# Moving one 128-column copy out of PSUM from ScalarE to VectorE in the opening of a layernorm, state-space and gated-MLP kernel

## The chip, the cores and the metric

One core of one Trainium2 chip. The metric is the device time of the kernel in microseconds (us). Each timed comparison runs a kernel and the kernel before in turn on the same chip. A ratio is the mean time of one kernel's fast runs over the mean of the other's of the same rounds, with a 95% interval, so it is not quite the ratio of the medians quoted beside it. "Same" means within 2%.

## The reference

2048 rows of 512 bf16 values are normalised; the result feeds a diagonal state-space layer (A) and a gated MLP (B), and everything is added to the input.

```python
def _B_ref(x, w_gate, w_up, w_down):
    return (_gelu(x @ w_gate) * (x @ w_up)) @ w_down
x = A_x
xn = _layernorm(x, axis=-1)
return x + _A_ref(xn, ...) + _B_ref(xn, B_w_gate, B_w_up, B_w_down)
```

## The kernel before

The kernel builds a list of operations with estimated durations; a list scheduler orders VectorE, ScalarE and GpSimd by them, while TensorE and the sync queue run in the order of the program. The change lies in the first 5 us. To start TensorE early, the kernel doesn't normalise the first three tiles of 128 rows before the gate and up products. It subtracts a mean ("centring"), turns the centred tile by TensorE transposes into PSUM, copies it to SBUF, multiplies, and applies the scale afterwards. A tile's first turn (128 columns) has its own copy, so that the products of weight block k = 0 can start before the other three turns.

```python
def cent_T(j, k0, k1, bank):
    pt = PS[bank].bitcast(BF16)[:, 0:128 * (k1 - k0)]
    ...                                                # f: TensorE transposes of XN[j] into pt
    PE(f, 56.0 * (k1 - k0), [XNp[j][k0 > 0] if j < 2 else XN[j], IDN], [BANK[bank]], "T0")
    ...
    GATE["evTA"] = ACT(lambda e: e.activation(dst, src, ACTF.Copy), ...)     # the copy, on ScalarE
...
ch(cent(0, 0), cent(0, 1))         # VectorE, tile 0 (ch: keep this order on the engine)
cent_T(0, 0, 1, 7)                 # first turn of tile 0 and its copy
ch(cent(1, 0), cent(1, 1))         # VectorE, tile 1
fill(1)                            # one filler matmul
cent_T(0, 1, 4, 5)                 # the other three turns of tile 0
ks(0, 0, [0], True)                # gate products, block 0, tile 0
cent_T(1, 0, 1, 6)                 # first turn of tile 1
ks(0, 0, [1])                      # up products, block 0, tile 0
cent_T(1, 1, 4, 7)
ks(0, 1, [0], True); ks(0, 1, [1])
```

The weights come in blocks of 128 KB on the sync queue: gate 0, up 0, gate 1, up 1 and so on. Activation tiles 1 and 2 come on ScalarE's queue meanwhile.

## Time and profile before

| | before |
|---|---|
| median of the three runs known at first | 177.22 us (176.98 to 177.30) |
| profiled run, its span | 176.79 us, 175.5 us |
| TensorE / VectorE / ScalarE busy | 98% / 91% / 55% |

The span runs from the first to the last instruction. The prediction shows the engines' line, the chain of waits of the opening and the copy. Two more rows, from the page's 40 equal slices (4.4 us each): the granted TensorE clock in tenths, and the busy share of the 16 DMA engines.

```profile
PEclk9999999999999999999999999999999999999999
DMA  5999999794996000002025000002001000000321
```

The DMA engines are busy nine tenths or more in nine of the eleven slices from the second to the twelfth, and a finer view of this trace gives a busy share of 0.99 to 1.05 for each microsecond from 2 to 5 us, though whether the loads slow each other there is not shown. The clock row shows nothing but nines, although the first matmuls are twice as far apart as the later ones (427 against 216 ns for 512 columns); the starts of the matmuls have to be read for that. Below, "half clock" and "full clock" mean these two paces, and "release" the change from the first to the second.

### The profile page before, as it was taken

Reading aid. Unit: us, or ns where it says so; the run is one execution under the profiler, and the core shown is the slowest. Engines: PE = TensorE matmul, PEld = TensorE weight load, DVE = VectorE, ACT = ScalarE, POOL = GpSimd, SP = SyncE. Lnnn points to the kernel's source line nnn. Section 1 sums busy time; section 2 is a strip of 40 time slices with the busy share of each in tenths; the row PEclk is TensorE's granted clock in tenths of the full one; section 3 lists DMA queues with packets and bytes.
Section 4 is the critical chain, followed back from the end, with each engine's and each line's share of the span. In section 5 each row is a group of like instructions: output and inputs, shape, how many; then the busy total and the mean of one; then the engine's idle time right before and its main releaser. Section 6 shows DMA issues by size and latency. Waiting matters only on the chain.

```text
span 175.5 us, 2521 instructions
## 1 busy us (share of the span) xinstructions
PE 172.7 (98%) x889; PEld 84.9 (48%) x889; DVE 159.6 (91%) x279; ACT 95.9 (55%) x187; POOL 10.7 (6%) x24
## 2 busy tenths in 40 slices
PE   8999999999999999999999999999999999999995
PEld 2646464845544444444644444444454444444453
DVE  5987999997989989799899999989999899999931
ACT  5476778999767898484576792000667960000000
POOL 3212220220000000002100000000000000000000
PEclk9999999999999999999999999999999999999999
DMA  5999999794996000002025000002001000000321
GB/s 173 258 326 198 206 191 166 137 136 95 235 299 170 4 0 2 0 30 90 4 50 102 0 0 0 4 0 90 30 0 30 4 0 0 0 0 0 99 87 58
DMA packets 32420, 14.36 MB, mean 82 GB/s; under 512 B 23736, under 2 KB 32408, under 8 KB 32408
## 3 DMA queue, kind: packets, MB, share of 16 engines
q1 hardware_dynamic: 32096, 13.94, 35.0%
q10 hardware_dynamic: 312, 0.27, 0.6%
q8 instruction: 7, 0.11, 0.3%
q14 instruction: 5, 0.04, 0.1%
HBM read 6.46 MB, written 2.10 MB: 49 GB/s over the span
## 4 chain that ended last, share of the span: by engine, by line
PE 98%; DVE 0%; issue 0%
PE PS L880 37%; PE PS L839 32%; PE PS L745 16%; PE PS L708 4%; PE PS L697 3%; PE PS L813 3%; PE PS L929 2%; PE PS L680 1%; DVE arena L898 0%; PE PS L936 0%
## 5 line engine op out<-in xcount | busy, mean ns | idle before, releaser
L880 PE MATMUL PS<-arena 128*128 128x512 bf16 (+3 forms) x323 | 66.2, 366 | 0.0
L839 PE MATMUL PS<-arena 128*128 128x512 bf16 x264 | 58.1, 379 | 0.0
L880 PEld LDWEIGHTS PS<-arena 128*128 128x128 bf16 (+1 forms) x323 | 30.8, 98 | 35.2
L839 PEld LDWEIGHTS PS<-arena 128*128 128x128 bf16 x264 | 25.8, 98 | 30.2
L783 DVE TENSOR_TENSOR_SCAN arena<-arena 128x512 bf16<-128x512 f32 x32 | 38.8, 1252 | 0.0
L854 ACT ACTIVATE arena<-PS 128x512 bf16<-128x512 f32 x33 | 19.8, 599 | 26.2 <-DVE arena L898 16.7
L745 PE MATMUL PS<-arena 128*128 128x512 bf16 (+1 forms) x144 | 28.2, 355 | 0.0
L858 ACT ACTIVATE arena<-PS 128x512 bf16<-128x512 f32 x33 | 19.8, 599 | 5.4 <-PE PS L839 5.4
L745 PEld LDWEIGHTS PS<-arena 128*128 128x128 bf16 x144 | 14.1, 98 | 13.3
L872 ACT ACTIVATE PS<-arena 128x512 f32<-128x512 bf16 (+2 forms) x17 | 9.6, 581 | 19.7 <-DVE arena L898 19.0
L754 ACT ACTIVATE arena<-PS 128x512 bf16<-128x512 f32 x32 | 17.5, 595 | 1.8 <-PE PS L745 1.8
L898 DVE TENSOR_TENSOR arena<-PS,arena 128x512 bf16<-128x512 f32 (+2 forms) x17 | 10.9, 652 | 6.4 <-PE PS L880 6.3
L860 DVE TENSOR_TENSOR arena<-arena 128x512 bf16<-128x512 bf16 x33 | 13.1, 415 | 2.3 <-ACT arena L858 2.0
L772 DVE TENSOR_TENSOR arena<-arena 128x4096 bf16<-128x4096 bf16 (+1 forms) x5 | 9.2, 1857 | 0.4 <-ACT arena L607 0.4
L795 DVE TENSOR_TENSOR arena<-arena 128x4096 bf16<-128x4096 bf16 x4 | 9.2, 2290 | 0.1
L770 DVE TENSOR_TENSOR arena<-arena 128x4096 bf16<-128x4096 bf16 (+1 forms) x5 | 9.2, 1856 | 0.0
L796 DVE TENSOR_TENSOR arena<-arena 128x4096 bf16<-128x4096 bf16 x4 | 9.1, 2285 | 0.0
L717 ACT ACTIVATE arena<-PS,arena 128x256 bf16<-128x256 f32 (+1 forms) x16 | 6.5, 449 | 4.1 <-PE PS L697 2.4
L611 DVE BATCH_NORM_STATS2 arena<-arena 128x6 f32<-128x512 bf16 x12 | 7.7, 680 | 0.1
L708 PE MATMUL PS<-arena 128*128 128x512 bf16 (+1 forms) x40 | 7.1, 336 | 0.0
L720 DVE SCALAR_TENSOR_TENSOR arena<-PS,arena 128x256 bf16<-128x256 f32 (+1 forms) x16 | 6.3, 443 | 0.4 <-PE PS L697 0.4
L697 PE MATMUL PS<-arena 128*128 128x512 bf16 (+1 forms) x30 | 6.3, 350 | 0.0
(95 smaller groups left out, 124.2 us busy)
## 6 DMA issues: line engine op xcount, KB each, us to landing
out_dram<-arena SPq DMA_DIRECT2D x15, 128.0 KB, 1.7
arena<-in_A_x_dram SPq DMA_DIRECT2D x3, 512.0 KB, 5.8
arena<-in_B_w_down_dram SPq DMA_DIRECT2D x1, 1280.0 KB, 7.1
arena<-in_B_w_gate_dram SPq DMA_DIRECT2D x4, 128.0 KB, 3.1
arena<-in_B_w_up_dram SPq DMA_DIRECT2D x4, 128.0 KB, 3.4
arena<-in_B_w_gate_dram SPq DMA_DIRECT2D x1, 480.0 KB, 6.4
arena<-in_B_w_up_dram SPq DMA_DIRECT2D x1, 480.0 KB, 7.2
arena<-arena SPq DMA_TRANSPOSE x25, 3.1
```

The lines of the kernel that those rows point to most:

```text
L697: PE(lambda e: e.matmul(dst, XCd(j, k), WGU[:, ws[0]:ws[-1] + 1, k, f0:f1], start=first, stop=k == KD - 1, skip_group_check=True), d_pe([w ...
L708: ins_ = e.matmul(dst, XCd(j, k), WGU[:, :, k, f0:f1], start=(k == 0), stop=(k == KD - 1))
L745: ins_ = e.matmul(PS[bank][:, 128 * j0:128 * j1], BBT[c][dk].ap[:, 128 * s:128 * (s + 1)], XNT[b].ap[:, dk, 128 * j0:128 * j1], start=(dk ...
L754: GATE["evBu"] = ACT(lambda e, bank=bank, k3=k3, s=s, c=c: e.activation(SSc[k3][s][c].ap, PS[bank][:, :], ACTF.Copy), d_act(512), [BANK[ba ...
L783: V(lambda e, g=g, rb=rb, init=init: e.tensor_tensor_scan(g.ap, rb, g.ap, init, ALU.mult, ALU.add), d_dve_scan(512), [g, PA[RRr]] + ([CARc ...
L839: ins_ = e.matmul(PS[bank][0:m, c0:c1], W.ap[:, dk, 128 * ft:128 * ft + m], XNT[b].ap[:, dk, c0:c1], start=(dk == 0), stop=(dk == KD - 1))
L854: GATE["last_gelu"] = ACT(lambda e, bg=bg, kk=kk, m=m: e.activation(GG[kk].ap[0:m, :], PS[bg][0:m, :], ACTF.Gelu_apprx_tanh), d_act(512), ...
L858: ACT(lambda e, bu=bu, kk=kk, m=m: e.activation(UPB[kk].ap[0:m, :], PS[bu][0:m, :], ACTF.Copy), d_act(512), [BANK[bu]], [UPB[kk]], "evU")
L860: V(lambda e, kk=kk, m=m, ft=ft, k2=k2: e.tensor_tensor(HTt[k2][ft].ap[0:m, :], GG[kk].ap[0:m, :], UPB[kk].ap[0:m, :], ALU.mult), d_dve_tt ...
L872: ACT(lambda e: e.activation(PS[bank][:, c0:c1], X[tt].ap[:, c0:c1], ACTF.Copy), d_act(c1 - c0), [X[tt]], [BANK[bank]], "seed")
L880: ins_ = e.matmul(PS[bank][:, c0:c1], l_[:, 128 * j:128 * (j + 1)], r_[:, c0:c1], start=False, stop=last and n == len(ops) - 1, skip_group ...
L898: V(lambda e: e.tensor_tensor(OUTB[ko].ap[:, c0:c1], PS[bank][:, c0:c1], XD[tt].ap[:, c0:c1], ALU.add), d_dve_1x(c1 - c0), [BANK[bank], XD ...
```

## The change

The intent: the first turn's copy stands between TensorE and its first useful product. VectorE is expected to do it sooner (the kernel's own estimates, which are constants in its code, are 187 ns against 297 on ScalarE), and it goes into VectorE's queue ahead of the centring of tile 1, not behind it.

```diff
-        def cent_T(j, k0, k1, bank):
+        def cent_T(j, k0, k1, bank, eng="A"):
...
+            if eng == "V":
+                return V(lambda e: e.tensor_copy(dst, src), 110 + 0.6 * 128 * (k1 - k0), [BANK[bank]], w, "evT")
             GATE["evTA"] = ACT(lambda e: e.activation(dst, src, ACTF.Copy), d_act(128 * (k1 - k0)), [BANK[bank]], w, "evT")
...
-        cent_T(0, 0, 1, 7)
+        ch(cent_T(0, 0, 1, 7, "V"))
         ch(cent(1, 0), cent(1, 1))
```

Two lines are added, so the changed kernel's L699 is the L697 of before, its L959 the L957, and its copies are L686 (VectorE) and L687 (ScalarE).

## The prediction

> **What bounds the kernel now.** I began with the summary page: engines, then the chain that ended last.
>
> ```profile
> PE 172.7 (98%) x889; PEld 84.9 (48%) x889; DVE 159.6 (91%) x279; ACT 95.9 (55%) x187; POOL 10.7 (6%) x24
> ...
> PE 98%; DVE 0%; issue 0%
> ```
>
> TensorE is busy for 98% of the span, and the chain that set the end is TensorE from start to finish. So another engine's saving counts only where TensorE waits for that engine. To find such places I took the start-to-start distances of all 889 matmuls in the trace and subtracted what each shape costs in the steady part (216 ns for 512 columns, 109 for 256, 56 for 128). All excess over 12 ns lies before 5.6 us. Most of it is not waiting: the seven warm-up matmuls are 427 ns apart (3.15 us for seven), and 128 columns take 107 ns until about 5.2 us. Two real holes are left, both in this part of the chain in order of time:
>
> ```profile
> 0.77 3.15 PE PS L929 x7
> 3.92 0.11 PE PS L680
> 4.03 0.11 PE PS L936
> 4.13 0.32 PE PS L680 x3
> 4.45 0.03 issue
> 4.48 0.59 PE PS L697 x2
> 5.07 0.11 PE PS L680
> 5.18 0.30 PE PS L697 x2
> 5.48 0.17 PE PS L680 x3
> 5.65 0.95 PE PS L697 x8
> ```
>
> L680 is the turn (transpose) of a centred tile, L936 one filler matmul, L697 the first gate and up matmuls, which need the turned tile out of PSUM. The chain prints modelled ends, so it shows the hole only as 0.03 us of "issue". By starts it is larger: the last turn of tile 0 starts at 4.145 us and takes 107 ns of the array, so the array is free at 4.252, while L697 starts at 4.487: 0.235 us. The timelines of ScalarE and of the weight loads show what ends it:
>
> ```profile
> 4.06 0.28 ACT L685 ACTIVATE arena<-PS 128x128 bf16<-128x128 bf16 x1
> 4.49 0.49 ACT L685 ACTIVATE arena<-PS 128x384 bf16<-128x384 bf16 x1
> ...
> 4.45 0.14 PEld L697 LDWEIGHTS PS<-arena 128*128 128x128 bf16 x2 [0.27 <-issue]
> ```
>
> The first copy (L685, 128 columns, the one that the change moves) runs 4.065 to 4.342. TensorE's sequencer sees its semaphore at 4.380, and L697's first weight load starts at 4.456. The view says "issue" because this load has two waits and the first sits in a separate sequencer instruction, but the first copy's end is what it waited for; the other wait, for the first gate weights, was met at 3.564 by their landing record. The second hole, 5.486 to 5.549 (0.06 us), is the same for tile 1, whose first turn starts at 4.865 and whose copy runs 5.216 to 5.493.
>
> [...]
>
> **The change part by part.** It takes the 128-column copy off ScalarE and puts a VectorE copy in the queue ahead of the two centring instructions of tile 1. TensorE's order is unchanged in full, and so are GpSimd's and the transfers'.
>
> Start: VectorE's previous instruction ends at 3.56 + 0.31 = 3.87, the turn at 3.718 + 0.311 = 4.029. From a matmul's end to the waiting instruction took 36 ns on ScalarE here and the same on VectorE at the kernel's end (173.513 to 173.549). So it starts at 4.065, exactly where ScalarE did.
>
> Duration: no bf16 read from PSUM by VectorE is in the trace, so I scale. These rows are mean ns of one:
>
> ```profile
> L957 DVE TENSOR_SCALAR arena<-arena 128x128 bf16<-128x128 bf16 x2 | 0.5, 254 | 0.3 <-ACT arena L951 0.2
> ...
> L898 DVE TENSOR_TENSOR arena<-PS,arena 128x128 bf16<-128x128 f32 x1 | 0.3, 291 | 0.1
> ```
>
> The addition from PSUM takes 291 ns for 128 columns and 682 for 512, so 1.02 ns a column and about 158 fixed. Additions of 512 bf16 columns from SBUF take 415, or 148 fixed at 0.52 a column. [...] At 2x it takes 158 + 67 = 225 ns, at 1x 158 + 133 = 291. I choose 2x at three in four[...]. The result comes 0.052 us sooner than from ScalarE, or 0.014 later. The way from semaphore to weight load keeps both waits and about 114 ns; a VectorE end reached a weight load in 55 ns (3.645 to 3.700) and a ScalarE end in 52 (5.493 to 5.545), so the engine makes no difference.
>
> How much reaches the end (2x case): L697 starts at 4.435, tile 1's first turn at 4.813, its ScalarE copy at 5.164 to 5.441, and the matmul after the second hole at 5.497 in place of 5.549. Between these lies the first up matmul. Its weights landed at 4.852 and its load started at 4.895, so it can start at about 4.926 (31 ns later, as the gate's did), against 4.920 asked of it. The array can therefore use nearly everything, and the few lost ns fall in the second hole, which shrinks from 0.06 to 0.04 us. The part before about 5.2 us runs at half clock[...], but it is the copy of tile 1 that sets the next start, and that moves in full. Sum: -0.05 us at 2x, +0.01 at 1x.
>
> What VectorE pays: tile 1's centring starts after the copy. Ops here overlap their successor by some 85 ns, so at 4.065 + 0.14 = 4.205 in place of 4.095, 0.11 us later, and its first part ends at 4.46. The turn of tile 1 loads at 4.654 now, 4.60 then; with 55 ns of release it is ready at 4.51. The next VectorE instruction, statistics of tile 2, waits for tile 2's landing at 4.620 and started at 4.643; the centring would let it go at 4.374 + 0.229 = 4.603. That wait swallows the delay whole, so VectorE's later chain doesn't move.
>
> **Rivals.**
>
> *The copy is slower on VectorE than on ScalarE* (1x, or more fixed cost). [...] Against it: 158 fixed as measured. [...]
>
> *Tile 1's turn becomes the wait*, because its centring queues behind the copy. For it: a slack of only 0.09 us in my numbers. Against it: the delay would have to be nearly double. Even then it costs what exceeds the slack, under 0.1 us, and it would move the end by that.
>
> *The scheduler's new order makes a wait later.* The static order shows ScalarE doing the copy of tile 3 ahead of the first gelu, VectorE doing three normalisations in a row around 10 us, and hidden-product multiplies and scans swapping places around 82 to 95 us. Before, TensorE had no later hole over 12 ns, so there is nothing to win there and something to lose. Against it: the tile-3 copy now comes earlier than the matmul that was loaded 51 ns after its end; the last turned block of the first four tiles landed at 15.7 us and is needed at 17.58, and VectorE's last chain ends at 161.2 us, some 3 us before TensorE needs it. I give it one in ten, with 0.1 to 0.6 us.
>
> *The full hole is gained*, 0.235 us, if the copy were free. It can't be: the copy still needs PSUM read, write and two semaphores.
>
> **Range and chances.** From 177.22: -0.05 x 0.75 and +0.01 x 0.25 make -0.035, and the reordering risk some +0.03 by 0.1 x 0.3. I predict 177.18 us. The three times of before spread by 0.32 us, many times the effect, so the range is theirs widened a little, upward for the new order: 176.85 to 177.50. Two per cent is 3.5 us, fifteen times the whole hole, so faster by that much is excluded in practice; slower needs a new stall of that size on TensorE, and nothing in the new order points to one. Chances: faster 0.003, same 0.99, slower 0.007.
>
> **What would show it.** In the changed kernel: a VectorE copy starting near 4.07 us of 0.22 to 0.23 us (0.29 says 1x); L697's first load near 4.40 in place of 4.456; tile 1's centring 0.1 us later but tile 2's statistics still at 4.64; the matmul after tile 1's turn at about 5.50; TensorE without a hole over 0.02 us after that. I am wrong if the copy ends later than 4.34, if tile 1's turn waits for its centring, or if a hole appears after 6 us where the order on VectorE or ScalarE changed.

The sum came to -0.05 us at 2x and +0.01 at 1x, weighted to -0.035, and to 177.18 us. "1x" and "2x" are 1.02 ns a column, as in the f32 additions from PSUM (291 ns for 128, 682 for 512), and half of that, as in the bf16 operations from SBUF (415, 682 and 1219 ns for 512, 1024 and 2048 columns: 0.52). That a bf16 copy out of PSUM would run at the second, at three in four, and have the addition's fixed part, was the estimate. That the full hole can't be gained was measured afterwards: in the changed kernel 0.038 us to the copy's start, 0.224 for the copy and 0.146 to the matmul are still there.

## The result, and the profile after

| | before | after |
|---|---|---|
| median of 6 runs each | 177.10 us (176.82 to 177.30) | 177.08 us (176.99 to 177.40) |
| ratio | | 1.0003 (0.999 to 1.0016): same |
| profiled run | 176.79 us | 177.40 us |
| turn ends to copy starts | 0.036 us | 0.038 us |
| copy | 277 ns, ScalarE | 224 ns, VectorE |
| turn ends to first gate matmul | 0.458 us | 0.408 us |

The time lies in the range and the copy does what was said. But the profiled run is slower by 0.6 us. The engines' line and the chain that ended last, by engine:

```profile
PE 171.5 (97%) x874; PEld 84.5 (48%) x889; DVE 160.3 (91%) x280; ACT 95.5 (54%) x186; POOL 9.8 (6%) x24
...
PE 95%; DMA 2%; issue 1%; SPq 0%; DVE 0%
```

Fifteen matmul records are missing (874, but 889 weight loads), so TensorE's busy time can't be compared. New is the DMA in the chain. In order of time, the chain names it:

```profile
1.66 4.05 DMA arena<-in_B_w_up_dram
5.72 0.04 issue
5.76 0.39 PE PS L699 x2
6.15 0.17 PE PS L680 x3
```

The chain no longer passes through the turn or the copy. It comes from the load of the first up weights, issued at 1.66 and landed (complete, by its semaphore's record) at 5.72. In the kernel before they had landed at 4.85 and no chain showed them. The timeline of TensorE and its table of waits:

```profile
4.38 0.38 PE L699 MATMUL PS<-arena 128*128 128x256 bf16 x2
4.59 0.22 PE L680 MATMUL PS<-arena 128*128 128x128 bf16 x1
5.76 0.39 PE L699 MATMUL PS<-arena 128*128 128x256 bf16 x2 [0.95 <-DMA arena<-in_B_w_up_dram]
...
PE PS L699 <- DMA arena<-in_B_w_up_dram: 1.0, 1, 1.0
```

The gate matmuls start at 4.38 and tile 1's first turn at 4.59; then TensorE waits for a landing until 5.76. VectorE in the same stretch:

```profile
4.01 0.22 DVE L686 COPY arena<-PS 128x128 bf16<-128x128 bf16 x1
4.15 0.47 DVE L959 TENSOR_SCALAR arena<-arena 128x128 bf16<-128x128 bf16 x2
5.55 0.69 DVE L611 BATCH_NORM_STATS2 arena<-arena 128x6 f32<-128x512 bf16 x1 [0.93 <-DMA arena<-in_A_x_dram]
```

The copy, tile 1's centring behind it, and then a wait for tile 2's landing (0.93 us) that is much longer than the centring's delay (0.11 us, against the trace of before).

Is the lateness the change's doing, or does it vary between executions? And what of the new order later on? On the second: from the start of the 101st weight load (18.6 to 19.7 us) to the start of the last matmul it took 154.523 us in the trace of before and 154.522 in that of after. The same holds within 0.001 us for eleven of the experiment traces, and for the twelfth, warm_1, counted from its 95th load, since it has six warm-up matmuls fewer. The earlier part of the new order lies between the first 512-column matmul and the 101st load, which took 12.115 to 12.116 us in before and in all three traces of after. In these traces the reordered VectorE and ScalarE work costs and gains nothing, and all difference between runs is made before the 101st load, apart from 2.05 to 2.22 us from the last matmul's start to the end of the span.

### The profile page after: what moved, and what is told of

Same layout as the page of the kernel before. It is cut to its first block, busy times and chain, and to the rows that moved or that the text cites. A ratio compares the mean times of both kernels' runs of the same rounds, so it can differ in the third digit from the quotient of the medians.

```text
span 176.1 us, 2500 instructions
## 1 busy us (share of the span) xinstructions
PE 171.5 (97%) x874; PEld 84.5 (48%) x889; DVE 160.3 (91%) x280; ACT 95.5 (54%) x186; POOL 9.8 (6%) x24
## 4 chain that ended last, share of the span: by engine, by line
PE 95%; DMA 2%; issue 1%; SPq 0%; DVE 0%
PE PS L882 37%; PE PS L841 32%; PE PS L747 16%; PE PS L710 4%; PE PS L815 3%; PE PS L699 3%; DMA arena<-in_B_w_up_dram 2%; PE PS L680 0%; SPq L484 0%; SPq L493 0%; DVE arena L900 0%
## 5 line engine op out<-in xcount | busy, mean ns | idle before, releaser
L841 PE MATMUL PS<-arena 128*128 128x512 bf16 x257 | 57.1, 379 | 0.4
L856 ACT ACTIVATE arena<-PS 128x512 bf16<-128x512 f32 x33 | 19.7, 598 | 25.0 <-DVE arena L900 16.7
L874 ACT ACTIVATE PS<-arena 128x512 f32<-128x512 bf16 (+2 forms) x17 | 9.6, 582 | 19.7 <-DVE arena L900 19.0
L699 PE MATMUL PS<-arena 128*128 128x512 bf16 (+1 forms) x30 | 6.0, 337 | 1.0 <-DMA arena<-in_B_w_up_dram 1.0
```

The lines of the kernel that those rows point to most:

```text
L699: PE(lambda e: e.matmul(dst, XCd(j, k), WGU[:, ws[0]:ws[-1] + 1, k, f0:f1], start=first, stop=k == KD - 1, skip_group_check=True), d_pe([w ...
L841: ins_ = e.matmul(PS[bank][0:m, c0:c1], W.ap[:, dk, 128 * ft:128 * ft + m], XNT[b].ap[:, dk, c0:c1], start=(dk == 0), stop=(dk == KD - 1))
L856: GATE["last_gelu"] = ACT(lambda e, bg=bg, kk=kk, m=m: e.activation(GG[kk].ap[0:m, :], PS[bg][0:m, :], ACTF.Gelu_apprx_tanh), d_act(512), ...
L874: ACT(lambda e: e.activation(PS[bank][:, c0:c1], X[tt].ap[:, c0:c1], ACTF.Copy), d_act(c1 - c0), [X[tt]], [BANK[bank]], "seed")
```

## The experiments

In the tables, "stretch" is the time from the start of tile 0's first turn to the first 512-column matmul: 25 matmuls, which need 2.04 us at full clock without a wait (13 of 55.8 ns and 12 of 109.2). "Full clock" is the start of the first matmul whose record is within 30 ns of the short duration; those before it are of half-clock length, the last one sometimes in between. Starts and landings are from the traces' records; like the prediction's, they count from a point 3 ns before that of the views.

### The same two kernels again

`rep_before` and `pair_before` are the kernel before, `rep_after` and `pair_after` the changed one, with no edit.

> The kernel before, unchanged, timed against itself: it shows how far a ratio strays with no change at all, and gives a second profile of it. Theory (the landing of the first up weights sets when TensorE's stream starts, and varies from execution to execution): ratio 1.000 within 0.002; the first up weights land between 4.8 and 5.8 us, and the profiled time is 176.8 us plus about as much as they land later than 4.85. Rival (landings are steady, and the 0.6 us between the two profiles came from the change): they land at 4.85 within 0.1, and the profiled time is 176.8 within 0.15.

> The changed kernel, unchanged. Theory: ratio 1.000 within 0.002, copy 0.22 us, and a landing of the first up weights that has nothing to do with the change: anywhere from 4.8 to 5.8 us, time 176.75 us plus what it lands later than 4.85. Rival (the change costs time by itself): weights land at 5.7 again and the ratio is 1.002 to 1.004.

> The kernel before once more, a third profile of it. Theory: from the end of tile 0's first turn to the first gate matmul 0.458 us as in the other two; the up weights' landing and the clock's release fall anew; ratio 1.000 within 0.002; the profiled time follows the start of the 101st weight load with 158.0 us between them, less 0.15 if the last store is quick. Rival: the 0.458 is chance.

> The changed kernel once more, a third profile. Theory: 0.408 us from the end of the turn to the first gate matmul, 0.050 less than before, and no trace of it in the time: ratio 1.000 within 0.002. Rival (the gain reaches the end): 0.9997, which these rounds can't tell from 1.000; rival (the change costs): 1.002 or more.

| profile | turn ends to first gate matmul | up weights landed | full clock | stretch | profiled time | median and ratio |
|---|---|---|---|---|---|---|
| before | 0.458 | 4.85 | 5.19 | 2.94 | 176.79 | |
| rep_before | 0.458 | 5.44 | 5.84 | 3.27 | 177.59 | 177.35, 1.0008 (0.999 to 1.0026) |
| pair_before | 0.457 | 4.81 | 3.93 | 2.68 | 177.19 | 177.13, 0.9995 (0.9975 to 1.0016) |
| after | 0.408 | 5.72 | 3.74 | 3.52 | 177.40 | 177.08, 1.0003 (0.999 to 1.0016) |
| rep_after | 0.408 | 5.50 | 5.55 | 3.32 | 177.21 | 177.19, 1.0003 (0.9985 to 1.002) |
| pair_after | 0.408 | 5.59 | 6.35 | 3.68 | 177.62 | 177.33, 1.0014 (0.9993 to 1.0035) |

The first column repeats to 0.001 us: 0.050 us is what the change gains at its own place. The timelines of rep_before and then rep_after show the two ways:

```profile
4.16 0.28 ACT L685 ACTIVATE arena<-PS 128x128 bf16<-128x128 bf16 x1
4.58 0.37 PE L697 MATMUL PS<-arena 128*128 128x256 bf16 x1
```

```profile
4.06 0.23 DVE L686 COPY arena<-PS 128x128 bf16<-128x128 bf16 x1 [0.17 <-PE PS L680]
4.43 0.59 PE L699 MATMUL PS<-arena 128*128 128x256 bf16 x2
```

The up weights land anywhere from 4.81 to 5.72 us, and also late with no change at all (5.44 in rep_before), so the rival with steady landings falls. In all three profiles of the changed kernel TensorE waits for them, for 0.63 to 1.11 us beyond the preceding turn's time on the array, far more than 0.050. In the profiles of before it was 0, 0.42 and 0.10. The profiled time less the start of the 101st weight load is 158.01 to 158.05 us in these six, so the opening accounts for the rest. It isn't the stretch alone: rep_before lost another 0.35 us where tile 3, landed at 8.87, held its turn, and pair_before 0.27 near 8.8 us and 0.38 at 17.6, there for a turned block that landed at 17.94. And my own rule in the expectations, 176.8 us (176.75 for after) plus the lateness of the landing, is a miss: it gives 177.39 for rep_before and 177.40 for rep_after, measured 177.59 and 177.21, and pair_before took 177.19 with the earliest landing of the six.

One thing stays open. All three landings of after are later than all three of before, which has a chance of 1 in 20 if the kernel doesn't matter. The copy can't have caused the part of the lag that is there by 4.0 us, before or as it starts: the DMA records of after then already had fewer KB completed than those of before, taken in pairs (504, 511, 575 against 594, 568, 634). And in the later experiments with the same order of loads the groups mix: the first up weights landed at 5.03 to 5.31 in six traces with the VectorE copy, inside the range of before, and at 5.29 in noW_S, with the ScalarE copy. Nor do the timed runs follow: pooled over all rounds, the changed kernel's 18 average 177.26 us (standard deviation 0.24), the 50 of before 177.19 (0.29, one run of 179.28 left out). With 0.07 us of standard error on the difference, neither a gain of 0.05 nor a loss of 0.2 is quite excluded.

### Without any wait for the weights

`noW_S` (copies on ScalarE) and `noW_V` (first copy on VectorE) stream a constant in place of the weights in the first three tiles' early products. The results are wrong; the loads still run.

```diff
+            mov = nc.const_aps.tensor(1.0, (128, 512), BF16)[:, 0:w * len(ws)].rearrange("p (w f) -> p w f", w=len(ws))
-            PE(lambda e: e.matmul(dst, XCd(j, k), WGU[:, ws[0]:ws[-1] + 1, k, f0:f1], ...),
-               ..., [(WGc, WUc)[w_][k] for w_ in ws] + [XCs[j][k > 0]] + ...)
+            PE(lambda e: e.matmul(dst, XCd(j, k), mov, ...),
+               ..., [XCs[j][k > 0]] + ...)
```

> Wrong results on purpose: the matmuls of the first three tiles' first blocks stream a constant in place of the gate and up weights, so none of them waits for a landing; copies on ScalarE as before. Theory: no hole of TensorE ends with a weight landing; the hole before the first gate matmul stays at 0.1 to 0.25 us and that before tile 1's matmuls at about 0.06; the time falls by the mean lateness of the weights, 0 to 0.8 us, to 176.5 to 177.0, and its spread shrinks. Rival (weights never bound in most executions): time within 0.1 us of before.

> The same, wrong on purpose too, with the first copy on VectorE. Against the one with ScalarE. Theory: with the weights out of the way the 0.05 us (277 ns on ScalarE against 224 on VectorE) is seen whole in the trace, the first matmul starting about 0.34 us after the end of tile 0's first turn in place of 0.40, and in the times as 0.05 us at most, which 5 rounds may just not resolve. Rival (the full hole of 0.2 us was to be had): 0.15 us or more less than the one with ScalarE.

Measured: noW_S 177.27 us, ratio 0.9999 (0.998 to 1.0018); noW_V 177.17 us, ratio 1.0002 (0.998 to 1.0025), both against the kernel before. The weight loads of TensorE, noW_S and then noW_V:

```profile
4.44 0.13 PEld L698 LDWEIGHTS PS<-const-bfloat16-1.0,arena 128*128 128x128 bf16 x2 [0.19 <-ACT arena L685]
```

```profile
4.34 0.13 PEld L700 LDWEIGHTS PS<-const-bfloat16-1.0,arena 128*128 128x128 bf16 x2 [0.16 <-DVE arena L686]
```

From the end of the turn to the matmul it is 0.369 and 0.319 us (I had expected 0.40 and 0.34), the same 0.050. (With one wait fewer, the load follows the copy's end by about 0.05 us. In the kernel before it was 0.114, with a wait in TensorE's sequencer, 4.377 to 4.428 us in the views' count, in between; here the views name the copy itself as what ended the load's idle time.) The trace half of the expectation holds in the main: no wait ends with a landing of these weights, though the small hole before tile 1's matmuls in noW_S is 0 and not 0.06 us. The time half is a miss: the waits are gone, yet the times did not fall to 176.5 to 177.0, and those of noW_V spread from 176.65 to 177.94. The intervals, 0.3 to 0.4 us either way, could hide a fall of 0.17 us, the mean of the three waits of before, so the times alone don't refute my theory, nor do they decide on the rival's 0.15 us between the two kernels. But in the trace of noW_S the stretch took 3.32 us without any such wait, longer than the 2.68 to 3.27 of the kernel before with them, so the landings alone do not set the opening. The tile 1 turns in TensorE's timeline show why, noW_S and then noW_V:

```profile
5.38 0.53 PE L680 MATMUL PS<-arena 128*128 128x128 bf16 x3
```

```profile
4.92 0.33 PE L680 MATMUL PS<-arena 128*128 128x128 bf16 x3
```

Three turns take 0.53 us in one and 0.33 in the other: TensorE was still at half clock in noW_S, until 6.34 us, and at full clock from 4.53 in noW_V. The profiled times are 177.37 and 176.65. So a second thing varies: the moment at which the clock is released. The two losses overlap: in after, at full clock from 3.74 us, TensorE was free for the up products at 4.65 and waited 1.11 us for them; in rep_after, at half clock until 5.55, it was free at 4.92 and waited 0.63, of which difference the earlier landing (5.50 against 5.72) makes 0.22 and the later arrival the rest.

### The clock by itself

`warm_1` is the changed kernel with `nwarm = 1` in place of `nwarm = 7`: one warm-up matmul, then an idle array (2.35 us in the timeline) up to the first turn, which starts at 3.71 us, as in the kernel before (3.74 in after).

> The changed kernel with one warm-up matmul in place of seven, so the array is idle from 1.2 to 3.7 us and its clock is released later. Theory (the moment of the release, 3.7 to 6.3 us in the runs so far, is the second thing that sets the opening): release 7 us or later, 1.0 to 2.2 us more, ratio 1.006 to 1.0125. Rival (the landings alone set the opening): under 0.5 us more.

Measured: 178.74 us (177.40 to 179.72), ratio 1.0081 (1.0041 to 1.0121). The first full-clock matmul starts at 9.38 us, and the stretch is 4.39 us. TensorE's timeline:

```profile
5.97 1.91 PE L699 MATMUL PS<-arena 128*128 128x256 bf16 x8
7.67 0.63 PE L680 MATMUL PS<-arena 128*128 128x128 bf16 x4
```

Eight matmuls of 256 columns in 1.91 us; in the kernel before, the same eight took 1.05 in this view (from 5.55). The moment of release is worth more than anything else found here, 1.4 us on average between this case and the usual one. The theory with two causes, landings and release, is the one that stands; how they add up in each execution is not worked out here.

### The copy later

`behind` queues the VectorE copy after tile 1's centring. The copy is created by a function that is called there; nothing else differs.

```diff
-        ch(cent_T(0, 0, 1, 7, "V"))
+        first_copy = cent_T(0, 0, 1, 7, "V")
         ch(cent(1, 0), cent(1, 1))
+        ch(first_copy())
```

> The copy stays on VectorE but is queued behind the centring of tile 1, not ahead of it. It should start near 4.49 us in place of 4.07 and let the first gate matmul go near 4.87 in place of 4.44. Theory (the first up weights' landing, 4.85 to 5.72 us so far, comes after the copy in most executions and hides it): that wait shrinks by what the copy is later, so the stream loses 0 to 0.45 us in the trace and the ratio to before is 1.000 to 1.002. Rival (the copy is what TensorE's stream hangs on): the full 0.4 us, ratio 1.0025 or more.

`dose_x3` and `dose_x8` put two and seven copies of the same block into unused scratch ahead of the real one. The 0.14 us that the expectations reckon for each is the distance in the trace of after from the start of the copy to that of the next VectorE instruction (4.01 to 4.15 in the view above).

```diff
-                return V(lambda e: e.tensor_copy(dst, src), ...)
+                def many(e):
+                    for i in range(2):                 # 7 in dose_x8
+                        e.tensor_copy(HT[0].ap[:, i:i + 1, 0:128], src)
+                    return e.tensor_copy(dst, src)
+                return V(many, ...)
```

> Two more copies of the same block into unused scratch ahead of the real one on VectorE: the first block out of PSUM comes about 0.28 us later (0.14 each). Theory: hidden behind the up weights wherever they land later than about 5.15 us, so 0 to 0.25 us; ratio 1.000 to 1.0015. Rival (on the path in full): 0.28 us always.

> Seven more copies, about 0.98 us later. Theory: longer than the wait for the up weights covers, and tile 2's statistics are pushed behind it as well, so now it shows, but by less than its length: 0.2 to 0.8 us, ratio 1.001 to 1.0045. Rival (in full): 1.0 us, ratio 1.0055 or more. Rival (nothing in the opening reaches the end): ratio 1.000. In all three of these kernels the time from the 101st weight load to the end of the span should be 156.72 us within 0.03, as in the six runs so far.

| | first gate matmul | up weights landed | full clock | stretch | profiled time | median and ratio |
|---|---|---|---|---|---|---|
| behind | 4.81 | 5.31 | 6.29 | 3.57 | 177.28 | 176.90, 0.9986 (0.9968 to 1.0005) |
| dose_x3 | 4.70 | 5.31 | 3.92 | 3.14 | 176.84 | 176.86, 0.9988 (0.9967 to 1.0009) |
| dose_x8 | 5.35 | 5.03 | 4.14 | 3.55 | 177.28 | 177.28, 1.0037 (0.9998 to 1.0075) |

TensorE's waits, in behind, dose_x3 and dose_x8 in turn:

```profile
PE PS L699 <- DVE arena L686: 0.4, 1, 0.4
```

```profile
PE PS L703 <- DVE arena L689: 0.4, 1, 0.4
PE PS L703 <- DMA arena<-in_B_w_up_dram: 0.2, 1, 0.2
```

```profile
PE PS L703 <- DVE arena L689: 1.0, 1, 1.0
```

In dose_x3 the first gate matmul starts 0.26 us later than in rep_after, and the up products still start with their landing (5.36, landing 5.31): the delay is hidden in full. In behind, the gate matmul is 0.37 us later and the wait for the up weights is down to 0.06 us; it is almost used up, and the timed runs show no loss. That the block went behind the centring instead of ahead thus cost nothing that can be measured, and its ratio even lies below the range I gave, with an interval that contains 1. In dose_x8 nothing hides the copy any more: the weights have been there since 5.03 and the chain passes through the copies. Four of its six runs took 177.26 to 177.28 us, unusually alike, as if the copies and no longer the landings set them; the other two took 178.71 and 179.27, and I have no trace of those. The kernel before had one such run in 51 (179.28), and warm_1, with the release at 9.38 us in its trace, took 177.40 to 179.72; whether the release was late here is not shown. The median is 0.1 us above that of before, below the expected 0.2 to 0.8; the ratio with the two long runs is inside it, but its interval reaches 1. So the copy's place binds the end only when it is later by several tenths of a microsecond, and this is a reading of traces; the times alone would not carry it. One part of the last expectation is a miss: from the 101st weight load to the end of the span the three kernels took 156.57 to 156.58 us, not 156.72. The 0.14 us lie behind the last matmul, whose start is 2.05 to 2.06 us before the end here and was 2.19 to 2.22 in the six runs meant; why, no run here shows.

### Shortening the wait for the up weights

`early_up` loads tile 2 on the sync queue after the first gate and up blocks, and turns tile 2 later; one block of tile 0's products moves up.

```diff
-        GATE["par"] = S.order_behind(ld_x0(2, "scalar"), GATE["par"])
...
+            if k == 1:
+                ld_x0(2)
...
-        cent_T(2, 0, 1, 6)
-        cent_T(2, 1, 4, 7)
         ks(1, 1, [0, 1])
+        cent_T(2, 0, 1, 6)
+        cent_T(2, 1, 4, 7)
+        ks(2, 0, [0, 1])
         ks(0, 2, [0, 1], True)
...
-        for j in range(3):
+        for j in range(1, 3):
             ks(2, j, [0, 1])
```

> The changed kernel with the load of activation tile 2 moved from ScalarE's queue to behind the first gate and up weights on the sync queue, and tile 2's turn moved behind tile 1's second block: 128 KB less stand ahead of the first up weights. Theory: they land about 0.4 us earlier than in the other runs, 4.4 to 5.2, the wait of TensorE for them falls under 0.3 us, and the time by 0 to 0.5 us if tile 2, now landing at 5 to 5.7, does not hold the stream in turn: ratio 0.997 to 1.000. Rival (the order of loads is indifferent, landings are late at random): no change of the landing and ratio 1.000.

The 0.4 us agree with the trace of before: 128 KB at the 318 GB/s that were moved in it from 2 to 3 us would take 0.41.

Measured: 177.17 us, ratio 0.9997 (0.9977 to 1.0016). The first up block landed at 4.69, within what I expected and earlier than in the other thirteen traces (4.81 to 5.72), and the wait for it was only 0.09 us; tile 2 landed behind it, at 5.06. One trace, but it speaks against the rival. But the wait came back further on. TensorE's waits:

```profile
PE PS L700 <- DMA arena<-in_B_w_up_dram: 1.0, 2, 0.6
```

These are for the second up block (landed 6.37) and the fourth (10.06). By 7 us between 1382 and 1438 KB had been completed in each of the other thirteen traces, and 1346 KB here: this order of the loads did not bring more in. That all transfers together are the limit is not shown, since in this trace the DMA engines were busy only 0.61 of the time from 3 to 4 us.

`up_late` moves tile 1's other turns and its gate products ahead of the first up products.

```diff
         cent_T(1, 0, 1, 6)
-        ks(0, 0, [1])
         cent_T(1, 1, 4, 7)
         ks(0, 1, [0], True)
+        ks(0, 0, [1])
         ks(0, 1, [1])
```

> The changed kernel with tile 1's three remaining turns and its two gate matmuls moved ahead of the first up matmuls on TensorE, so that work which needs no up weights fills the wait for them. Theory (that wait is real lost time): the wait falls from 0.4 to 1.0 us to 0.3 or less and the following second-block matmuls start up to 0.25 us sooner unless the second gate block's landing (5.2 to 6.3 us) holds them; where the up weights land early it can lose up to 0.2. Ratio 0.998 to 1.0005. Rival (the wait is an artefact of the trace): 1.000, no start moves.

Measured: 176.90 us, ratio 0.999 (0.9966 to 1.0013). The up weights landed at 5.28 and held nothing. In TensorE's timeline another wait has taken their place:

```profile
5.52 1.26 PE L699 MATMUL PS<-arena 128*128 128x256 bf16 x10 [0.20 <-ACT arena L687]
```

TensorE now waits for ScalarE's copy of tile 1's first turn, until 5.52. The stretch is 3.03 us, shorter than in any trace of the changed kernel, but 2.68 and 2.94 occurred in those of before with early landings. Whether it beats both kernels can't be told from these rounds, and I don't claim it.

## Why the prediction was right, and where it was not

- **The place of the copy, its start, length and way to TensorE**: right. It started 0.036 to 0.038 us after the turn's end in all three traces of after, took 224 to 225 ns as scaled for 2x, and the gate matmul followed 0.146 us after its end, as after ScalarE's. The gain at this place is 0.050 us against 0.052 predicted.
- **Tile 1's centring 0.11 us later, hidden by tile 2's landing**: right. Counted from the turn's end it started 0.177 to 0.180 us later, against 0.058 to 0.100 before. Tile 2's statistics did not start until 5.33 to 5.55 us, when its load had landed, not at 4.64. That the landing hid the delay is partly luck: in pair_before tile 2 landed at 4.25 and the statistics started at 4.48, as soon as the centring let them, so there VectorE's chain would have moved.
- **How much reaches the end**: this step had the wrong premise. I took the up weights' 4.852 us as fixed and found a few nanoseconds of conflict. The landing varies over 0.9 us, and in the three traces of the changed kernel it came after everything that the copy could speed up, so the predicted -0.05 us was swallowed there. The first gate matmul of tile 1, announced for about 5.50, started at 5.94 to 6.35, behind the hole of 0.63 to 1.11 us before the first up matmul. With the landings of the three traces of before I estimate from their starts that the full 0.05 us would have passed in the one that I had, about 0.035 in pair_before (where tile 1's copy, not the up weights, ended the last hole) and nothing in rep_before. No timed run can show that. I had the conflicting load in hand, with 6 ns between "asked for" and "possible", and should have read such a margin as a coin's toss.
- **The clock's release at about 5.2 us**: taken from one trace as it stood. It came between 3.74 and 6.35 us in the traces with seven warm-up matmuls, and with the landings the stretch ran from 2.68 to 3.68 us in the six of the repeats, more than the 0.3 us spread that I put into the range. That the range was taken from the spread and not from the effect is what made it hold.
- **The new order later**: right that it costs nothing; 154.522 to 154.523 us in every trace. One figure there was wrong: the last turned block of the first four tiles landed at 16.19 us, not at 15.7 (I had taken the third of four). The slack is thinner than told, and pair_before, which is the kernel before, waited 0.38 us for that block.
- **Copy slower on VectorE; tile 1's turn becomes the wait; the full hole gained**: none occurred. The turn of tile 1 followed the gate matmuls without a wait in all three traces.
- **Its sums**: two slips, both too small to matter. The +0.03 us for the reordering is named but not added: with it 177.22 - 0.035 + 0.03 is 177.21 or 177.22, not 177.18. And with its own 1.02 ns a column the fixed part of the addition is 160 to 161 ns, not 158, which makes the copy 227 or 228 ns; the 225 that came true owes 2 or 3 ns to the slip. That the fixed part of an f32 addition holds for a bf16 copy was an assumption.

"Same" was thus right because the whole hole was 0.235 us of 177, and the sign of the small gain was never put to a test that the times could pass.

## What to carry to other kernels

A wait that one trace shows in the opening may be there in one execution and replaced by another in the next (here the same 128 KB load, issued at 1.66 us, landed between 4.81 and 5.72 us in six profiles of two kernels); before a gain is counted through such a chain, ask which inputs of the following steps land within a few hundred nanoseconds of being needed, and take a second profile of the unchanged kernel. Where TensorE is full, measure a fixed late interval first (here the 101st weight load to the last matmul): if it is constant, all of the question lies in front of it. A change of 50 ns is to be judged in the trace, at its own place, when executions differ by 300.
